# An attention-and-mixing kernel: first batch reordered, u of batch 0 transposed by TensorE, attention woven into nine tenths of mixing

## The chip, the cores and the metric

The kernel runs on one core of a Trainium2 chip. The metric is the device time of one execution in microseconds (us). Most quoted profiles are single executions; their span, from the first to the last instruction, is about 2 us shorter than the time. A run is called fast when it is within 1.5% of the fastest run of the same kernel, slow otherwise.

Engines: TensorE (PE in the profile; its weight loads are PEld), VectorE (DVE), ScalarE (ACT), GpSimd (POOL, here it only issues the loads), SyncE (SP, here it issues output writes and transposes by DMA).

## The reference

Two stages on 4 batches. First attention with 8 heads of 64 over 768 positions, where a query sees the previous 96 positions and the first 8. Then a mixing block on its result x (768 x 512):

```python
theta = x @ w_theta
zr, zi = x * cos(theta), x * sin(theta)
y = einsum('ts,bsd->btd', w_tok_r, zr) + einsum('ts,bsd->btd', w_tok_i, zi)
u = x + y
out = u + maximum(u @ w_ch, 0)
```

## The kernel before

Work comes in tiles of 128 positions (NT = 6 per batch), heads in pairs (NP = 4). `prep` copies a pair's q and k and transposes them on TensorE; `scores` multiplies, exponentiates (ScalarE) and applies a bias table (VectorE); `values` makes x; `xtrans` transposes x; `theta` gives cosine, sine and z; `mix` is the large product (12 matmuls for each of 6 tiles); `utrans` transposes u; `chan` multiplies by w_ch, adds and writes; `trans_w(tt)` transposes the token weights of tile tt; `warm` multiplies zeros, only to keep TensorE's clock up. The attention of batch b+1 is woven into `mix` of batch b. From batch 1 on, x is transposed by DMA; u is transposed by DMA in all batches but for the very last tile.

```python
    # head, VectorE and ScalarE in this order: ramp, ident, dist, the 8 bias tables,
    # e_bufs, grel, gbias, gmask, shift, halfpi, ... (cut)
    etab = const.tile([T, H, W], BF)
    for h in range(H):
        nc.scalar.activation(etab[:, h, :], dist, AF.Exp, scale=-slopes[h])
    # ... (cut)
    def utrans(b, tt):
        u = u_sb[b, tt]
        uT = moe.tile([T, NC, T], BF, name="uT", bufs=4)
        uTs[(b, tt)] = uT
        if (b, tt) != (B - 1, NT - 1):
            nc.sync.dma_start_transpose(out=uT, in_=u)
            return
        ps = ps_small([T, NC, T], BF)
        for dc in range(NC):
            nc.tensor.transpose(ps[:, dc, :], u[:, dc * T:(dc + 1) * T], ident)
        nc.scalar.copy(out=uT, in_=ps)
    # ... (cut)
    load_w()
    load_all(1)
    with tc.manual_schedule(engines={mybir.EngineType.PE}):
        warm(8)
        prep(0, 0)
        warm(2)
        for p in range(1, NP):
            prep(0, p)
            for c in range(NT // 2):
                scores(0, p - 1, c)
                warm(1)
        # ... globals_, vglob, last scores (cut)
        for p in range(NP):
            values(0, p, 0)
            values(0, p, 1)
            if p:
                trans_w(p - 1, nc.scalar.copy)
                xtrans(0, p - 1, nc.scalar.copy)
        trans_w(3, nc.scalar.copy)
        xtrans(0, NP - 1, nc.scalar.copy)
    tail = []
    for b in range(B):
        # ... (cut)
        th[2:2] = tail                 # thetas, with the last chans of batch b-1
        if b:
            th[3:3] = pre              # and the q/k preparation of batch b+1
            pre = []
        weave(th, [])
        # main: mix, with utrans(tt-1) and chan(tt-2) after the first third of tile tt (cut)
        weave(main, pre + side, 0.3 if b == 0 else 0.0)
        tail = [(512, lambda b=b: utrans(b, NT - 1)), (2048, lambda b=b: chan(b, NT - 2)),
                (2048, lambda b=b: chan(b, NT - 1))]
```

Only the head fixes TensorE's order by hand. After it the order is the scheduler's, which may move instructions; the order of this text is a wish.

The softmax here doesn't subtract the row's maximum and nothing guards it: scores larger than these inputs give would overflow.

Of the kernel before, what the change touches and what calls it, by code (L numbers as in the profile page):

```python
# [16 lines left out]
def kernel(  # L17
# [15 lines left out]
    T = 128  # L33
# [29 lines left out]
    def alloc_loads(b):  # L63
        qk = ld.tile([T, 2, H, NT, D], BF, name="qk")
        vn = ld.tile([T, H, NT, D + 1], BF, name="vn")
        nc.vector.memset(vn[:, :, :, D:D + 1], 1.0)
        loads[b] = (qk, vn)
# [17 lines left out]
    load_v(0, 0, 4)  # L85
    load_v(0, 4, 4)

    ones = const.tile([T, W], FP)
# [14 lines left out]
    far = const.tile([T, W], FP)  # L103
    nc.vector.tensor_scalar(far, dist, 0.0, 1e6, op0=ALU.is_lt, op1=ALU.mult)
    nc.vector.tensor_add(dist, dist, far)
    nc.vector.tensor_scalar(far, dist, float(NL), 1e6, op0=ALU.is_ge, op1=ALU.mult)
    nc.vector.tensor_add(dist, dist, far)
    etab = const.tile([T, H, W], BF)
    for h in range(H):
        nc.scalar.activation(etab[:, h, :], dist, AF.Exp, scale=-slopes[h])  # L110


    NE = 4
    e_bufs = []
    for i_ in range(NE):
        e_t = const.tile([T, 2, NT, 2 * T], BF, name=f"e_{i_}")
        nc.vector.memset(e_t[:, :, :, W:2 * T], 0.0)
        e_bufs.append(e_t)
    e_cnt = [0]



    grel = const.tile([T, T], FP)
    nc.vector.tensor_scalar(grel, ramp[:, 0:T], kmod[:, 0:1], None, op0=ALU.subtract)
    gbias = const.tile([T, 2], FP)
    for hh in range(2):
        for p in range(NP):
            nc.vector.memset(gbias[GS * p:GS * (p + 1), hh:hh + 1], -float(NL) * slopes[2 * p + hh])

    gneg = const.tile([T, 1], FP)  # L130
    nc.vector.tensor_scalar(gneg, grel[:, 0:1], -float(NG), -30000.0, op0=ALU.is_le, op1=ALU.mult)
    nc.vector.tensor_scalar(gbias, gbias, gneg, None, op0=ALU.add)

    gfar = const.tile([T, T], FP)
    nc.vector.tensor_scalar(gfar, grel, float(NL), None, op0=ALU.is_ge)
    gmask = const.tile([T, T], BF)
    nc.vector.scalar_tensor_tensor(gmask, in0=grel, scalar=0.0, in1=gfar, op0=ALU.is_lt, op1=ALU.add)

    shift = const.tile([T, NP, T], BF)
    nc.vector.memset(shift, 0.0)  # L140
    for p in range(NP):
        nc.vector.tensor_copy(out=shift[0:NG, p, GS * p:GS * p + NG], in_=ident[0:NG, 0:NG])

    halfpi = const.tile([T, 1], FP)
    nc.vector.memset(halfpi, HALF_PI)

# [23 lines left out]

    zero = const.tile([T, 512], BF)
    nc.vector.memset(zero, 0.0)  # L172

    def warm(n):
# [14 lines left out]

    def prep(b, p):  # L190
        qk = loads[b][0]
# [5 lines left out]
        with behind("dve"):  # L197
            for i_ in range(2):
                nc.vector.tensor_copy(out=qkn[:, :, i_].rearrange("p t h d -> p h t d"),  # L199
                                      in_=qk[:, i_, 2 * p:2 * p + 2])  # L200
        qT = att.tile([T, S], BF, name="qT", bufs=6)
        kT = att.tile([T, S], BF, name="kT", bufs=6)
        for i_, dst in ((0, qT), (1, kT)):
            ps = ps_small([T, NT, T], BF)
            with behind("pe"):
                for t_ in range(NT):
                    nc.tensor.transpose(ps[:, t_, :], qkn[:, t_, i_].rearrange("p h d -> p (h d)"), ident)  # L207

            dst = dst.rearrange("p (n t) -> p n t", t=NT)
            src = ps.rearrange("p t n -> p n t")  # L210
            if i_ == 0:
                nc.vector.tensor_copy(out=dst, in_=src)  # L212
            else:
                nc.scalar.copy(out=dst, in_=src)  # L214
        qkT[(b, p)] = (qT, kT)

# [18 lines left out]
    def scores(b, p, c):  # L235
# [21 lines left out]
        else:  # L257
            nc.scalar.activation(e_t[:, :, jt, 0:W], pb[:, :, 0:W], AF.Exp, scale=scale)
            nc.scalar.activation(e_t[:, :, jt + 1, 0:T], pb[:, :, W:W + T], AF.Exp, scale=scale)
            nc.vector.tensor_mul(e_t[:, :, jt, 0:W], e_t[:, :, jt, 0:W], etab[:, 2 * p:2 * p + 2, :])  # L260
# [79 lines left out]
    def mix(b, tt, g):  # L340
# [8 lines left out]
        if g == NT // 2 - 1:  # L349
            u_sb[b, tt] = moe.tile([T, DM], BF, name="u", bufs=4)  # L350
            anchor["dve"] = nc.vector.tensor_add(  # L351
                u_sb[b, tt].rearrange("p (g d) -> p g d", g=NP), x_sb[b][:, :, tt, :],
                ps.rearrange("p (g d) -> p g d", g=NP)).ins

    def utrans(b, tt):
        u = u_sb[b, tt]
        uT = moe.tile([T, NC, T], BF, name="uT", bufs=4)
        uTs[(b, tt)] = uT
        if (b, tt) != (B - 1, NT - 1):
            nc.sync.dma_start_transpose(out=uT, in_=u)  # L360
            return
# [43 lines left out]

    def weave(main, side, s0=0.0):

# [3 lines left out]
        for w, f in main:  # L411
            f()
            done += w
            while i_ < len(side) and s0 + (1 - s0) * (sdone + side[i_][0] / 2) / stot <= done / total:
                side[i_][1]()
                sdone += side[i_][0]
                i_ += 1
# [6 lines left out]
    with tc.manual_schedule(engines={mybir.EngineType.PE}):  # L424
        warm(8)
        prep(0, 0)
        warm(2)
        for p in range(1, NP):
            prep(0, p)
            for c in range(NT // 2):  # L430
# [3 lines left out]
        for p in range(NP):  # L434
            vglob(0, p)
        for c in range(NT // 2):
            scores(0, NP - 1, c)
            warm(1)
        for p in range(NP):
            values(0, p, 0)  # L440
            values(0, p, 1)
            if p:
                trans_w(p - 1, nc.scalar.copy)
                xtrans(0, p - 1, nc.scalar.copy)
        trans_w(3, nc.scalar.copy)
        xtrans(0, NP - 1, nc.scalar.copy)
    tail = []
    for b in range(B):
        nxt = b + 1 if b + 1 < B else None
        if b + 2 < B:  # L450
            load_all(b + 2)
        th = [(2048, lambda c=c, j=j: theta(b, c, j)) for c in range(NT // 2) for j in range(2)]
        th[2:2] = tail
        pre = [(1536, lambda p=p: prep(nxt, p)) for p in range(NP)] if nxt else []
        if b:
            th[3:3] = pre
            pre = []
        weave(th, [])
        main = []
        for tt in range(NT):  # L460
            for g in range(NT // 2):
                main.append((2048, lambda tt=tt, g=g: mix(b, tt, g)))
                if b == 0 and g == 1 and tt < 2:
                    main.append((1536, lambda tt=tt: trans_w(tt + 4)))
                if tt and g == 0:
                    main.append((0, lambda tt=tt: utrans(b, tt - 1)))
                if tt > 1 and g == 0:
                    main.append((2048, lambda tt=tt: chan(b, tt - 2)))
        side = attention_steps(nxt) if nxt else []
        weave(main, pre + side, 0.3 if b == 0 else 0.0)  # L470
        tail = [(512, lambda b=b: utrans(b, NT - 1)), (2048, lambda b=b: chan(b, NT - 2)),
                (2048, lambda b=b: chan(b, NT - 1))]
    for _, f in tail:
        f()
# [35 lines left out]
```

## Time and profile before

| | before |
|---|---|
| median of its first runs | 201.2 us |
| span of the profiled run | 199.5 us |
| TensorE busy | 173.0 us, 87% |
| head, to the first mixing matmul | 40.35 us |
| mixing 0 | 39.64 us |
| theta of batch 1, 2 | 12.39, 12.40 us |
| mixing 1, 2 | 29.18, 29.54 us |
| theta of batch 3, to the end | 36.00 us |

The stretches end where the first theta matmul or the first mixing matmul of a batch starts in the timeline. This is the view of busy time by stretches for the kernel before: start and end, length, then for each engine busy time and (instructions); then the granted TensorE clock (1 is full), the mean number in which DMA engines were busy, and GB/s.

```profile
core 0: us, PE busy (x) PEld busy (x) DVE busy (x) ACT busy (x) POOL busy (x), PEclk, DMA share, GB/s
0.00:40.35 40.35, 28.83 (x363) 17.61 (x363) 28.44 (x92) 27.13 (x46) 21.43 (x28) 1.00 1.37 175
40.35:79.99 39.64, 35.62 (x372) 18.68 (x373) 28.16 (x62) 21.45 (x32) 3.57 (x3) 1.00 1.77 180
79.99:92.38 12.39, 10.56 (x82) 5.52 (x81) 11.25 (x24) 7.68 (x9) 2.22 (x1) 1.00 1.94 133
92.38:121.56 29.18, 29.18 (x293) 13.63 (x292) 19.62 (x43) 16.71 (x26) 0.00 (x0) 1.00 0.34 89
121.56:133.96 12.40, 10.32 (x82) 5.64 (x81) 9.68 (x20) 7.01 (x8) 0.00 (x0) 1.00 0.34 48
133.96:163.50 29.54, 29.43 (x294) 13.77 (x292) 20.09 (x43) 17.17 (x27) 0.00 (x0) 1.00 0.38 81
163.50:171.12 7.62, 5.69 (x26) 2.19 (x25) 3.02 (x6) 2.91 (x3) 0.00 (x0) 1.00 0.47 116
171.12:199.50 28.38, 23.37 (x108) 10.03 (x107) 12.35 (x23) 4.93 (x6) 0.00 (x0) 1.00 0.28 86
```

Mixing 1 and 2 have TensorE busy all the time. The idle time is in the head, in mixing 0, in the theta stretches and at the end. The Trainium skill, "Perfetto Trace Analysis", Identifying the Most-Contended Engine, warns that matmul busy time is no measure of headroom because matmuls are pipelined. This trace agrees that they are: a 128x512 matmul is shown 380 ns long, but in a dense stretch the next one starts 0.216 us later. So work is better counted in starts: 0.86 us for a chan.

TensorE's waits, longest in total first (line and tile that waited, what it waited for, us in total, times, longest):

```profile
PE ps L177 <- DVE zero L172: 7.8, 1, 7.8
PE ps L371 <- DMA uT<-u: 3.3, 4, 2.1
PE pb L327 <- DMA xT<-x_sb: 3.0, 2, 1.9
PE ps L207 <- DVE qkn L199: 2.0, 2, 1.1
```

L371 is `chan`, L327 is `theta`, L207 is `prep`. The timeline shows the two DMA waits (start, length, engine, line, operation, count, and in brackets the idle time before it and its releaser; lines from two places of the same timeline):

```profile
7.89 0.84 DVE L199 COPY qkn<-qk 128x768 bf16<-128x768 bf16 x1
14.23 1.73 ACT L251 ACTIVATE e_115<-pb 128x896 bf16<-128x896 f32 x2
...
47.10 3.85 SPq L360 DMA_TRANSPOSE uT<-u  x2
54.46 1.04 PE L371 MATMUL ps<-w_ch_bf,uT 128*128 128x512 bf16 x4 [2.07 <-DMA uT<-u]
...
122.15 1.21 SPq L306 DMA_TRANSPOSE xT<-x_sb  x1
126.42 0.82 PE L327 MATMUL pb<-w_theta_bf,xT 128*128 128x512 bf16 x3 [1.91 <-DMA xT<-x_sb]
```

The first u transpose is issued at 47.10 and lands 7.3 us later, although the median of all u transposes is 2.5 us: from about 5 to 80 us the loads keep the DMA engines at 160 to 210 GB/s. The last x transpose of batch 2 is issued when mixing 1 has already ended, and theta waits for it.

### The profile page before, as it was taken

To read this page: it belongs to the slowest core of one execution; us is meant where nothing else is said; L and a number is where in the kernel's file an instruction comes from. 1 tells how busy PE (TensorE), PEld (TensorE's weight loads), DVE (VectorE), ACT (ScalarE), POOL (GpSimd) and SP (SyncE) were. 2 spreads that over 40 slices of the span, in tenths; PEclk is the share of its full clock that TensorE was granted. 3 is DMA by queue.
4 is the path that set the end of the run, shared out by engine and by line. 5 is a ranking of instruction groups with operands and counts; after the bars stand their busy time and mean duration, and the time that the engine had idled before them with its cause. 6 is when DMAs were issued, how large, how long until landed. Compare 5 with 4: busy or idle time off the path is not lost.

```text
span 199.5 us, 3940 instructions
## 1 busy us (share of the span) xinstructions
PE 173.0 (87%) x1610; PEld 87.1 (44%) x1610; DVE 132.6 (66%) x305; ACT 105.0 (53%) x153; POOL 27.2 (14%) x31
## 2 busy tenths in 40 slices
PE   0498789998599899799999999699999997899981
PEld 0154268443353445453345455443444552344430
DVE  7878678177765686996676777677686661753332
ACT  2449956990359553189964431399845312920010
POOL 7991461040110000400000000000000000000000
PEclk9999999999999999999999999999999999999999
DMA  4999999999999999699114437210233845103432
GB/s 66 161 174 168 210 209 206 205 176 166 194 165 188 210 162 183 116 135 138 30 26 118 122 92 108 40 69 37 55 82 100 111 120 123 53 20 100 130 91 105
DMA packets 61345, 24.76 MB, mean 124 GB/s; under 512 B 47504, under 2 KB 58256, under 8 KB 61328
## 3 DMA queue, kind: packets, MB, share of 16 engines
q0 software_dynamic: 35760, 12.85, 66.0%
q1 hardware_dynamic: 25568, 11.67, 26.8%
q8 instruction: 12, 0.20, 0.4%
q14 instruction: 5, 0.04, 0.1%
HBM read 25.69 MB, written 6.29 MB: 160 GB/s over the span
## 4 chain that ended last, share of the span: by engine, by line
PE 61%; DMA 13%; ACT 12%; DVE 9%; issue 3%; ACTq 0%
PE ps L346 27%; DMA uT<-u 11%; PE ps L371 9%; PE pb L327 6%; PE pb L292 6%; PE pb L247 4%; PE ps L207 3%; ACT kT L214 2%; DMA xT<-x_sb 2%; PE ps L177 2%; ACT cs L331 2%; DVE u L351 1%; ACT e_121 L251 1%; PE ps L292 1%; PE ps L167 1%
## 5 line engine op out<-in xcount | busy, mean ns | idle before, releaser
L346 PE MATMUL ps<-zri,w_tokT_151 128*128 128x512 bf16 x144 | 53.9, 380 | 1.2 <-DVE zri L335 1.2
L346 PE MATMUL ps<-zri,w_tokT_152 128*128 128x512 bf16 x144 | 54.0, 379 | 0.1
L374 DVE SCALAR_TENSOR_TENSOR o_sb<-ps,u 128x512 f32<-128x512 f32 x24 | 16.5, 688 | 18.8 <-PE ps L371 18.8
L371 PE MATMUL ps<-w_ch_bf,uT 128*128 128x512 bf16 x96 | 24.7, 379 | 4.1 <-DMA uT<-u 3.3
L327 PE MATMUL pb<-w_theta_bf,xT 128*128 128x512 bf16 x96 | 24.6, 379 | 3.3 <-DMA xT<-x_sb 3.0
L214 ACT COPY kT<-ps 128x768 bf16<-128x768 bf16 x16 | 12.4, 808 | 25.9 <-PE ps L207 25.9
L335 DVE TENSOR_TENSOR zri<-x_sb,cs 128x512 bf16<-128x512 bf16 x48 | 18.2, 421 | 8.8 <-ACT cs L331 7.2
L346 PEld LDWEIGHTS <-w_tokT_151 128*128 128x128 bf16 x144 | 14.0, 97 | 16.9 <-issue 4.4
L351 DVE TENSOR_TENSOR u<-x_sb,ps 128x512 bf16<-128x512 bf16 x24 | 16.4, 684 | 7.0 <-PE ps L346 6.7
L346 PEld LDWEIGHTS <-w_tokT_152 128*128 128x128 bf16 x144 | 14.0, 98 | 12.8 <-issue 2.0
L247 PE MATMUL pb<-qT,kT 64*128 64x224 bf16 x192 | 16.8, 254 | 1.7 <-ACT e_117 L251 0.5
L212 DVE COPY qT<-ps 128x768 bf16<-128x768 bf16 x16 | 14.9, 948 | 2.5 <-PE ps L207 2.5
L177 PE MATMUL ps<-zero 128*128 128x512 bf16 x22 | 8.9, 476 | 8.3 <-DVE zero L172 7.8
L207 PE MATMUL ps<-ident,qkn 128*128 128x128 bf16 x192 | 13.8, 223 | 2.0 <-DVE qkn L199 2.0
L78 POOL DMA_DIRECT2D vn<-in_v_dram x5 | 10.2, 2050 | 35.7 <-DVE rec L300 24.7
L327 PEld LDWEIGHTS <-xT 128*128 128x128 bf16 x96 | 8.8, 98 | 14.1 <-DMA xT<-x_sb 4.1
L207 PEld LDWEIGHTS <-qkn 128*128 128x128 bf16 x192 | 12.1, 100 | 6.4 <-DVE qkn L199 3.8
L371 PEld LDWEIGHTS <-uT 128*128 128x128 bf16 x96 | 8.2, 97 | 14.7 <-DMA uT<-u 6.0
L247 PEld LDWEIGHTS <-kT 64*128 64x128 bf16 x192 | 6.0, 94 | 18.2 <-issue 15.8
L331 ACT ACTIVATE cs<-pb,halfpi 128x1024 bf16<-128x1024 f32 x12 | 13.6, 1131 | 0.5 <-ACT cs L332 0.3
L332 ACT ACTIVATE cs<-pb 128x1024 bf16<-128x1024 f32 x12 | 12.5, 1039 | 0.0
L199 DVE COPY qkn<-qk 128x768 bf16<-128x768 bf16 x32 | 11.5, 411 | 0.8 <-DMA qk<-in_q_dram 0.5
(128 smaller groups left out, 261.8 us busy)
## 6 DMA issues: line engine op xcount, KB each, us to landing
out_dram<-o_sb SPq DMA_DIRECT2D x24, 256.0 KB, 2.2
qk<-in_q_dram POOLq DMA_DIRECT2D x3, 768.0 KB, 17.5
qk<-in_k_dram POOLq DMA_DIRECT2D x3, 768.0 KB, 21.8
vn<-in_v_dram POOLq DMA_DIRECT2D x3, 768.0 KB, 23.3
w_nat<-in_moe_w_tok_r_dram POOLq DMA_DIRECT2D x3, 384.0 KB, 14.7
w_nat<-in_moe_w_tok_i_dram POOLq DMA_DIRECT2D x3, 384.0 KB, 15.9
qk<-in_q_dram POOLq DMA_DIRECT2D x4, 192.0 KB, 5.6
qk<-in_k_dram POOLq DMA_DIRECT2D x4, 192.0 KB, 5.8
```

What stands on the lines that cost most here:

```text
L207: nc.tensor.transpose(ps[:, t_, :], qkn[:, t_, i_].rearrange("p h d -> p (h d)"), ident)
L212: nc.vector.tensor_copy(out=dst, in_=src)
L214: nc.scalar.copy(out=dst, in_=src)
L247: nc.tensor.matmul(pb[:, hh, j * W:j * W + n], lhsT=kT[R, jt * T:(jt + 1) * T], rhs=qT[R, jt * T:jt * T + n], start=True, stop=True)
L292: nc.tensor.matmul(o, lhsT=l_, rhs=r_, start=(i_ == 0), stop=(i_ == len(mms) - 1))
L327: nc.tensor.matmul(pb[:, j, :], lhsT=xT[:, dc, st * T:(st + 1) * T], rhs=w_theta_bf[:, dc, :], start=(dc == 0), stop=(dc == NC - 1))
L331: nc.scalar.activation(cs[:, 0], pb, AF.Sin, bias=halfpi)
L335: nc.vector.tensor_mul(zri[b][:, i_, 2 * c + j_, :].rearrange("p (g d) -> p g d", g=NP), xb[:, :, 2 * c + j_, :], cs[:, i_, j_].rearrange( ...
L346: anchor["pe"] = nc.tensor.matmul(ps, lhsT=w_tokT[wi][:, st, tt * T:(tt + 1) * T], rhs=zri[b][:, wi, st, :], start=(st == 0 and wi == 0), ...
L351: anchor["dve"] = nc.vector.tensor_add(u_sb[b, tt].rearrange("p (g d) -> p g d", g=NP), x_sb[b][:, :, tt, :], ps.rearrange("p (g d) -> p g ...
L371: nc.tensor.matmul(ps_c, lhsT=uT[:, dc, :], rhs=w_ch_bf[:, dc, :], start=(dc == 0), stop=(dc == NC - 1))
L374: nc.vector.scalar_tensor_tensor(o_sb, in0=ps_c, scalar=0.0, in1=u, op0=ALU.max, op1=ALU.add)
```

## The change

Its intent: start the first batch as soon as its first q/k has landed; take the weight transposes out of the head; keep u of batch 0 off the DMA queues while they are full of loads; let attention end before mixing does, so that the last x transpose is hidden; load ScalarE's sine table early; and reorder the boundary between batches. One q/k load buffer instead of two pays for a fifth u buffer.

```diff
-        qk = ld.tile([T, 2, H, NT, D], BF, name="qk")
+        qk = ld.tile([T, 2, H, NT, D], BF, name="qk", bufs=1)
 # ... constants and bias tables become functions, called between the preparations (cut)
-                nc.vector.tensor_copy(out=qkn[:, :, i_].rearrange("p t h d -> p h t d"),
-                                      in_=qk[:, i_, 2 * p:2 * p + 2])
+                (nc.scalar.copy if b == 0 and i_ and p < 2 else nc.vector.tensor_copy)(
+                    out=qkn[:, :, i_].rearrange("p t h d -> p h t d"), in_=qk[:, i_, 2 * p:2 * p + 2])
 # ... scores of the last pair end with a dummy sine:
+            if p == NP - 1:
+                with tc.issue_after(last):
+                    nc.scalar.activation(junk, halfpi, AF.Sin)
-        if (b, tt) != (B - 1, NT - 1):
+        if b and (b, tt) != (B - 1, NT - 1):
             nc.sync.dma_start_transpose(out=uT, in_=u)
-        prep(0, 0)
-        warm(2)
+        prep(0, 0, 4)
+        bias_table(0)
         for p in range(1, NP):
-            prep(0, p)
+            prep(0, p, 2 if p == 1 else 0)
+            bias_table(p)
+            if p == 1:
+                constants()
 # ... last scores go between the values; of trans_w only tile 0 stays in the head (cut)
-        th[2:2] = tail
-        if b:
-            th[3:3] = pre
+        elif nxt:
+            order = rest[:-1] + pre[:2] + th[:2] + pre[2:] + th[2:3] + rest[-1:] + th[3:]
+        else:
+            order = rest[:-1] + th[:3] + rest[-1:] + th[3:]
 # ... batch 0: trans_w(tt+1) and utrans(tt-1) after the second third of tile tt; later batches:
 # utrans(tt) right after tile tt (cut)
-        weave(main, pre + side, 0.3 if b == 0 else 0.0)
+        weave(main, side, 0.3 if b == 0 else 0.0, 0.9)
```

More of the change, by code (lines that the diff above doesn't have):

```diff
@@ L86 @@
     load_v(0, 4, 4)
+    zero = const.tile([T, 512], BF)
+    nc.vector.memset(zero, 0.0)
     ones = const.tile([T, W], FP)
@@ L103 @@
     far = const.tile([T, W], FP)
-    nc.vector.tensor_scalar(far, dist, 0.0, 1e6, op0=ALU.is_lt, op1=ALU.mult)
-    nc.vector.tensor_add(dist, dist, far)
-    nc.vector.tensor_scalar(far, dist, float(NL), 1e6, op0=ALU.is_ge, op1=ALU.mult)
-    nc.vector.tensor_add(dist, dist, far)
+    nc.vector.tensor_scalar(far, dist, 0.0, None, op0=ALU.is_lt)
+    nc.vector.scalar_tensor_tensor(far, in0=dist, scalar=float(NL), in1=far, op0=ALU.is_ge, op1=ALU.add)
+    nc.vector.scalar_tensor_tensor(dist, in0=far, scalar=1e6, in1=dist, op0=ALU.mult, op1=ALU.max)
@@ L108, with bias_table @@
     etab = const.tile([T, H, W], BF)
-    for h in range(H):
-        nc.scalar.activation(etab[:, h, :], dist, AF.Exp, scale=-slopes[h])
+    def bias_table(p):
+        for h in (2 * p, 2 * p + 1):
+            nc.scalar.activation(etab[:, h, :], dist, AF.Exp, scale=-slopes[h])
     NE = 4
-    e_bufs = []
-    for i_ in range(NE):
-        e_t = const.tile([T, 2, NT, 2 * T], BF, name=f"e_{i_}")
-        nc.vector.memset(e_t[:, :, :, W:2 * T], 0.0)
-        e_bufs.append(e_t)
+    e_bufs = [const.tile([T, 2, NT, 2 * T], BF, name=f"e_{i_}") for i_ in range(NE)]
@@ L119 @@
     e_cnt = [0]
-    grel = const.tile([T, T], FP)
-    nc.vector.tensor_scalar(grel, ramp[:, 0:T], kmod[:, 0:1], None, op0=ALU.subtract)
     gbias = const.tile([T, 2], FP)
-    for hh in range(2):
-        for p in range(NP):
-            nc.vector.memset(gbias[GS * p:GS * (p + 1), hh:hh + 1], -float(NL) * slopes[2 * p + hh])
-    gneg = const.tile([T, 1], FP)
-    nc.vector.tensor_scalar(gneg, grel[:, 0:1], -float(NG), -30000.0, op0=ALU.is_le, op1=ALU.mult)
-    nc.vector.tensor_scalar(gbias, gbias, gneg, None, op0=ALU.add)
@@ L134 @@
-    gfar = const.tile([T, T], FP)
-    nc.vector.tensor_scalar(gfar, grel, float(NL), None, op0=ALU.is_ge)
-    gmask = const.tile([T, T], BF)
-    nc.vector.scalar_tensor_tensor(gmask, in0=grel, scalar=0.0, in1=gfar, op0=ALU.is_lt, op1=ALU.add)
-    shift = const.tile([T, NP, T], BF)
-    nc.vector.memset(shift, 0.0)
-    for p in range(NP):
-        nc.vector.tensor_copy(out=shift[0:NG, p, GS * p:GS * p + NG], in_=ident[0:NG, 0:NG])
-    halfpi = const.tile([T, 1], FP)
-    nc.vector.memset(halfpi, HALF_PI)
+    gmask = const.tile([T, T], BF)
@@ new lines, with constants @@
+    shift = const.tile([T, NP, T], BF)
+    halfpi = const.tile([T, 1], FP)
+    junk = const.tile([T, 1], FP)
+    def constants():
+        for e_t in e_bufs:
+            nc.vector.memset(e_t[:, :, :, W:2 * T], 0.0)
+        grel = const.tile([T, T], FP, name="grel")
+        nc.vector.tensor_scalar(grel, ramp[:, 0:T], kmod[:, 0:1], None, op0=ALU.subtract)
+        for hh in range(2):
+            for p in range(NP):
+                nc.vector.memset(gbias[GS * p:GS * (p + 1), hh:hh + 1], -float(NL) * slopes[2 * p + hh])
+        gneg = const.tile([T, 1], FP, name="gneg")
+        nc.vector.tensor_scalar(gneg, grel[:, 0:1], -float(NG), -30000.0, op0=ALU.is_le, op1=ALU.mult)
+        nc.vector.tensor_scalar(gbias, gbias, gneg, None, op0=ALU.add)
+        gfar = const.tile([T, T], FP, name="gfar")
+        nc.vector.tensor_scalar(gfar, grel, float(NL), None, op0=ALU.is_ge)
+        nc.vector.scalar_tensor_tensor(gmask, in0=grel, scalar=0.0, in1=gfar, op0=ALU.is_lt, op1=ALU.add)
+        nc.vector.memset(shift, 0.0)
+        for p in range(NP):
+            nc.vector.tensor_copy(out=shift[0:NG, p, GS * p:GS * p + NG], in_=ident[0:NG, 0:NG])
+        nc.vector.memset(halfpi, HALF_PI)
@@ L168, in trans_w @@
             (copy if wi else nc.vector.tensor_copy)(out=w_tokT[wi][:, :, tt * T:(tt + 1) * T], in_=ps)
-    zero = const.tile([T, 512], BF)
-    nc.vector.memset(zero, 0.0)
     def warm(n):
@@ L188, in behind, with prep @@
         return tc.issue_after(anchor[eng]) if eng in anchor else nullcontext()
-    def prep(b, p):
+    def prep(b, p, w=0):
         qk = loads[b][0]
@@ L214, in prep @@
                 nc.scalar.copy(out=dst, in_=src)
+            if w:
+                warm(w)
         qkT[(b, p)] = (qT, kT)
@@ L258, in scores @@
             nc.scalar.activation(e_t[:, :, jt, 0:W], pb[:, :, 0:W], AF.Exp, scale=scale)
-            nc.scalar.activation(e_t[:, :, jt + 1, 0:T], pb[:, :, W:W + T], AF.Exp, scale=scale)
+            last = nc.scalar.activation(e_t[:, :, jt + 1, 0:T], pb[:, :, W:W + T], AF.Exp, scale=scale).ins
+            if p == NP - 1:
+                with tc.issue_after(last):
+                    nc.scalar.activation(junk, halfpi, AF.Sin)
             nc.vector.tensor_mul(e_t[:, :, jt, 0:W], e_t[:, :, jt, 0:W], etab[:, 2 * p:2 * p + 2, :])
@@ L349, in mix @@
         if g == NT // 2 - 1:
-            u_sb[b, tt] = moe.tile([T, DM], BF, name="u", bufs=4)
+            u_sb[b, tt] = moe.tile([T, DM], BF, name="u", bufs=5)
             anchor["dve"] = nc.vector.tensor_add(
@@ L404, in attention_steps, with weave @@
         return steps
-    def weave(main, side, s0=0.0):
+    def weave(main, side, s0=0.0, s1=1.0):
         total = float(sum(w for w, _ in main)) or 1.0
@@ L413, in weave @@
             done += w
-            while i_ < len(side) and s0 + (1 - s0) * (sdone + side[i_][0] / 2) / stot <= done / total:
+            while i_ < len(side) and s0 + (s1 - s0) * (sdone + side[i_][0] / 2) / stot <= done / total:
                 side[i_][1]()
@@ L435 @@
             vglob(0, p)
-        for c in range(NT // 2):
-            scores(0, NP - 1, c)
-            warm(1)
+        scores(0, NP - 1, 0)
         for p in range(NP):
@@ L441 @@
             values(0, p, 1)
+            if p < 2:
+                scores(0, NP - 1, p + 1)
             if p:
-                trans_w(p - 1, nc.scalar.copy)
                 xtrans(0, p - 1, nc.scalar.copy)
-        trans_w(3, nc.scalar.copy)
         xtrans(0, NP - 1, nc.scalar.copy)
-    tail = []
+        trans_w(0, nc.scalar.copy)
+    rest = []
     for b in range(B):
@@ L451 @@
             load_all(b + 2)
-        th = [(2048, lambda c=c, j=j: theta(b, c, j)) for c in range(NT // 2) for j in range(2)]
-        th[2:2] = tail
-        pre = [(1536, lambda p=p: prep(nxt, p)) for p in range(NP)] if nxt else []
-        if b:
-            th[3:3] = pre
-            pre = []
-        weave(th, [])
+        lag = 2
+        th = [lambda c=c, j=j: theta(b, c, j) for c in range(NT // 2) for j in range(2)]
+        pre = [lambda p=p: prep(nxt, p) for p in range(NP)] if nxt else []
+        if b == 0:
+            order = th
+        elif nxt:
+            order = rest[:-1] + pre[:2] + th[:2] + pre[2:] + th[2:3] + rest[-1:] + th[3:]
+        else:
+            order = rest[:-1] + th[:3] + rest[-1:] + th[3:]
+        for f in order:
+            f()
         main = []
@@ L462 @@
                 main.append((2048, lambda tt=tt, g=g: mix(b, tt, g)))
-                if b == 0 and g == 1 and tt < 2:
-                    main.append((1536, lambda tt=tt: trans_w(tt + 4)))
-                if tt and g == 0:
-                    main.append((0, lambda tt=tt: utrans(b, tt - 1)))
-                if tt > 1 and g == 0:
-                    main.append((2048, lambda tt=tt: chan(b, tt - 2)))
-        side = attention_steps(nxt) if nxt else []
-        weave(main, pre + side, 0.3 if b == 0 else 0.0)
-        tail = [(512, lambda b=b: utrans(b, NT - 1)), (2048, lambda b=b: chan(b, NT - 2)),
-                (2048, lambda b=b: chan(b, NT - 1))]
-    for _, f in tail:
+                if b == 0 and g == 1 and tt + 1 < NT:
+                    main.append((1536, lambda tt=tt: trans_w(tt + 1)))
+                if tt >= lag and g == 0:
+                    main.append((2048, lambda tt=tt: chan(b, tt - lag)))
+                if b == 0 and tt and g == 1:
+                    main.append((512, lambda tt=tt: utrans(b, tt - 1)))
+            if b:
+                main.append((0, lambda tt=tt: utrans(b, tt)))
+        side = [(1536, f) for f in pre] if b == 0 else []
+        side += attention_steps(nxt) if nxt else []
+        weave(main, side, 0.3 if b == 0 else 0.0, 0.9)
+        rest = [lambda tt=tt, b=b: chan(b, tt) for tt in range(NT - lag, NT)]
+        if b == 0:
+            rest.insert(1, lambda b=b: utrans(b, NT - 1))
+    for f in rest:
         f()
```

## The prediction

> **What bounds the kernel now.** From the 201.2 us runs I read a span of 199.5 us. The table by stretches splits it: first batch before mixing, 0 to 40.3 us, TensorE busy 28.8; mixing of batch 0 with attention of batch 1 woven in, 40.3 to 80.0, TensorE 35.6 of 39.7; theta of batch 1, 12.5 us; mixing 1, 28.7 of 28.7 busy; theta of batch 2, 12.2 of 14.4; mixing 2, 27.9 of 27.9; the end from 163.5, 29.1 of 36.0. So mixing 1 and 2 are bound by TensorE and can't shrink; everything to be won is in the first 80 us and in the two gaps and the end. The timeline shows them: scores of the first batch paced by ScalarE (a pair of heads every 3.04 us), theta waiting until 37.4 for xT copies queued behind the token-weight copies, u transposes by DMA that land after 7.3 and 8.7 us while loads fill the queues (later ones take 2.5), an xT transpose issued at 122.15 and awaited at 126.4, another at 164.1.
>
> **Head.** The first pair of q/k is copied as soon as it lands (about 7 us, estimate from 1.3 plus 5.6), half of it by ScalarE, instead of after all constants. But TensorE's eight warm-up matmuls now end near 5 us and it then waits for data; the Trainium skill, "TensorE: Matmul & The Clock Gate", HAM clock gate, says the clock falls back after about 3.4 us idle. The trace agrees that first matmuls are slow (0.43 us, later 0.22), so the extra warm matmuls cost about 0.43 each. The eight bias-table exponentials (0.29 us each) now sit inside ScalarE's chain. I expect the first scores exponential at about 13.8 (was 14.2), and the third pair to end no earlier than before. The gain comes after it: values start while the last scores run, three of four early weight transposes leave (twelve transposes and 0.65 us each, with 0.8 us ScalarE copies), and the sine table load (1.28 us) is paid before the copies. VectorE now paces: eight reciprocals and multiplies (0.63 each) plus last table products 1.9 from 25.5, then an xT copy: theta's rest starts at 33.8, first cosine at 35.3 instead of 38.7. About -3.4 us.
>
> **Mixing 0.** Adds three weight transposes (2.0 us TensorE, 3.3 VectorE copies) and six PE transposes of u (about 1.3 TensorE, 3.5 ScalarE); removes DMA waits of 2.1 and 0.75 us and some of the slack. After the first u I count 30.4 us TensorE work to theta 1, where 30.4 passed before; with VectorE fuller I allow 1.5 us new waits. Theta 1 near 77.5 (was 80.0): cumulative -2.5.
>
> **Later.** Attention ends at nine tenths of mixing, so the last xT transpose lands before theta: theta 2 about 12.6 instead of 14.4 us (-1.8); end stage about 1.8 shorter (theta 3 no longer waits 1.05 and 0.27, nor the sine load 1.28). One q/k buffer: batch 2's load issues near 48 us (was 28.8), but isn't needed until about 76; batch 3's not until 118. Free, by my count.
>
> Sum: -2.5 -0.2 -1.8 -1.8, about -6.5: **194.6 us**, range 191.3 to 198.5. Faster by over 2%: 0.8; within: 0.18; slower: 0.02.
>
> **Signs.** TensorE busy rises slightly; no u transpose by DMA before about 90; the weight-from-xT waits on DMA vanish; theta 2's stretch has TensorE above 95%; mixing 1 and 2 stay 28 us.
>
> **What would make it wrong.** Batch 1's q/k landing after 46 us; small-PSUM rotation in mixing 0 stalling TensorE behind VectorE or ScalarE copies by more than 3 us; a cold TensorE clock delaying the first scores; batch 2's q/k landing after 76.

## The result and the profile after

The changed kernel took 193.3 us (median of four runs, 192.08 to 194.72) against 201.4; ratio 0.9598, 95% interval 0.9528 to 0.9667. All ratios here are the mean time of one kernel's fast runs over that of the other's in the same rounds, so they are not quite the ratio of the medians quoted. The profiled run is the fastest of the four (192.08 us, span 190.0), so the 9.5 us between the two profiles are more than the 8 us between the medians.

| stretch | before | after | difference |
|---|---|---|---|
| head, to the first mixing matmul | 40.35 | 35.71 | -4.64 |
| mixing 0 | 39.64 | 41.73 | +2.09 |
| theta 1 and mixing 1 | 41.57 | 39.57 | -2.00 |
| theta 2 and mixing 2 | 41.94 | 40.17 | -1.77 |
| theta 3, mixing 3, end | 36.00 | 32.82 | -3.18 |
| sum | 199.50 | 190.00 | -9.50 |

Theta and mixing are summed because one chan of 0.86 us moved from behind to before the mark at which each theta starts. So 0.86 of the +2.09 of mixing 0, and 0.86 of the -3.18 at the end, are moved work; the two rows between lose one chan and gain another. The same view of stretches, of the changed kernel:

```profile
core 0: us, PE busy (x) PEld busy (x) DVE busy (x) ACT busy (x) POOL busy (x), PEclk, DMA share, GB/s
0.00:35.71 35.71, 28.43 (x332) 16.09 (x334) 25.12 (x86) 26.60 (x46) 21.26 (x26) 1.00 1.38 171
35.71:77.44 41.73, 40.28 (x435) 23.23 (x444) 33.54 (x72) 25.78 (x40) 3.96 (x3) 1.00 1.75 152
77.44:86.27 8.83, 8.70 (x72) 4.92 (x71) 7.94 (x19) 6.81 (x9) 1.75 (x2) 1.00 1.63 134
86.27:117.01 30.74, 30.25 (x293) 14.31 (x296) 21.12 (x45) 17.91 (x28) 0.00 (x0) 1.00 0.72 130
117.01:126.11 9.10, 8.99 (x75) 5.04 (x76) 8.92 (x20) 6.67 (x8) 0.00 (x0) 1.00 0.24 72
126.11:157.18 31.07, 30.15 (x292) 14.22 (x296) 20.57 (x42) 17.70 (x28) 0.00 (x0) 1.00 0.35 84
157.18:163.22 6.04, 6.04 (x29) 2.74 (x28) 3.05 (x7) 3.50 (x4) 0.00 (x0) 1.00 0.44 142
163.22:190.00 26.78, 21.56 (x99) 9.28 (x99) 11.00 (x20) 3.06 (x4) 0.00 (x0) 1.00 0.29 84
```

TensorE is now busy for 96% of mixing 0 and 98 to 100% of each theta stretch. Its waits, longest in total first; L177 is `warm`, L377 is now `chan`; no wait of theta for xT is left:

```profile
PE ps L177 <- DVE zero L88: 1.4, 1, 1.4
...
PE ps L377 <- DMA uT<-u: 0.6, 2, 0.4
```

The places in the timeline that answer to those shown of before:

```profile
4.73 0.39 DVE L199 COPY qkn<-qk 128x768 bf16<-128x768 bf16 x1 [1.52 <-DMA qk<-in_q_dram]
12.59 1.71 ACT L253 ACTIVATE e_108<-pb 128x896 bf16<-128x896 f32 x2
...
43.63 0.39 PE L370 MATMUL ps<-ident,u 128*128 128x128 bf16 x4
44.05 0.59 ACT L371 COPY uT<-ps 128x512 bf16<-128x512 bf16 x1 [3.88 <-PE ps L370]
...
114.83 1.21 SPq L312 DMA_TRANSPOSE xT<-x_sb  x1
117.01 0.38 PE L333 MATMUL pb<-w_theta_bf,xT 128*128 128x512 bf16 x1
```

The first copy starts 3.2 us earlier and the first scores exponential 1.6 us earlier. The first u is transposed and copied within about a microsecond, where the DMA took 7.3. The last x transpose of batch 2 now goes out 2.2 us before its theta starts. Of the prediction's signs four came true (TensorE busy 174.4 us against 173.0, the first u transpose by DMA at 90.87, no theta wait for xT, theta 2 busy for 99%); the fifth did not: mixing 1 and 2 are 30.74 and 31.07 us instead of 28, 0.86 of the growth by the moved chan.

### The profile page after: what moved, and what is told of

The parts are those of the page before. It is cut to its first block, busy times and chain, and to the rows that moved or that the text cites. A ratio compares the mean times of both kernels' runs of the same rounds, so it can differ in the third digit from the quotient of the medians.

```text
span 190.0 us, 3965 instructions
## 1 busy us (share of the span) xinstructions
PE 174.4 (92%) x1616; PEld 89.8 (47%) x1641; DVE 131.3 (69%) x305; ACT 108.0 (57%) x162; POOL 27.0 (14%) x31
## 4 chain that ended last, share of the span: by engine, by line
PE 65%; ACT 15%; DVE 8%; DMA 6%; issue 3%; POOL 1%; ACTq 0%; SPq 0%; POOLq 0%
PE ps L352 27%; PE ps L377 10%; PE pb L333 9%; PE pb L298 7%; PE pb L249 5%; DMA uT<-u 3%; PE ps L207 3%; DMA qk<-in_k_dram 3%; ACT cs L337 2%; ACT kT L214 2%; ACT e_108 L253 2%; PE ps L170 2%; DVE qT L212 1%; DVE qkn L199 1%; DVE zri L341 1%
## 5 line engine op out<-in xcount | busy, mean ns | idle before, releaser
L352 PE MATMUL ps<-zri,w_tokT_119 128*128 128x512 bf16 x136 | 51.6, 381 | 1.2 <-DVE zri L341 0.5
L352 PE MATMUL ps<-zri,w_tokT_120 128*128 128x512 bf16 x138 | 52.2, 379 | 0.5 <-issue 0.2
L377 PE MATMUL ps<-w_ch_bf,uT 128*128 128x512 bf16 x89 | 23.5, 380 | 1.2 <-DMA uT<-u 0.6
L333 PE MATMUL pb<-w_theta_bf,xT 128*128 128x512 bf16 x93 | 23.2, 379 | 0.2
L214 ACT COPY kT<-ps 128x768 bf16<-128x768 bf16 x16 | 12.9, 806 | 12.9 <-PE ps L207 12.8
L352 PEld LDWEIGHTS <-w_tokT_120 128*128 128x128 bf16 x144 | 14.1, 98 | 12.5 <-issue 1.4
L371 ACT COPY uT<-ps 128x512 bf16<-128x512 bf16 x7 | 4.1, 587 | 27.0 <-PE ps L370 27.0
L207 PE MATMUL ps<-ident,qkn 128*128 128x128 bf16 x192 | 15.0, 222 | 0.9 <-DVE ident L101 0.4
L78 POOL DMA_DIRECT2D vn<-in_v_dram x5 | 9.5, 1921 | 24.9 <-DVE rec L306 20.9
L377 PEld LDWEIGHTS <-uT 128*128 128x128 bf16 x96 | 8.1, 98 | 10.4 <-DMA uT<-u 2.1
L199 DVE COPY qkn<-qk 128x768 bf16<-128x768 bf16 x30 | 10.8, 387 | 3.1 <-DMA qk<-in_q_dram 3.1
L177 PE MATMUL ps<-zero 128*128 128x512 bf16 x28 | 10.4, 473 | 2.4 <-DVE zero L88 1.4
```

The costliest lines, as they stand in the source:

```text
L207: nc.tensor.transpose(ps[:, t_, :], qkn[:, t_, i_].rearrange("p h d -> p (h d)"), ident)
L214: nc.scalar.copy(out=dst, in_=src)
L333: nc.tensor.matmul(pb[:, j, :], lhsT=xT[:, dc, st * T:(st + 1) * T], rhs=w_theta_bf[:, dc, :], start=(dc == 0), stop=(dc == NC - 1))
L352: anchor["pe"] = nc.tensor.matmul(ps, lhsT=w_tokT[wi][:, st, tt * T:(tt + 1) * T], rhs=zri[b][:, wi, st, :], start=(st == 0 and wi == 0), ...
L377: nc.tensor.matmul(ps_c, lhsT=uT[:, dc, :], rhs=w_ch_bf[:, dc, :], start=(dc == 0), stop=(dc == NC - 1))
```

## The experiments

Twelve kernels ran, all correct. The table gathers them; ratios are to the kernel before in the same rounds. They ran in three groups (r0, e1, e2, e3; f1, e4, e5, e6, on another chip; h2, h3, i1, g2), so runs of different groups are compared by their ratios.

| run | what it is | fast mean, us | ratio | 95% interval |
|---|---|---|---|---|
| r0_after | changed kernel | 194.07 | 0.9601 | 0.9550 to 0.9653 |
| e1_u_by_dma | changed, u of batch 0 by DMA | 202.51 | 1.0019 | 0.9970 to 1.0068 |
| i1_dma_u_two_qk | the same, two q/k buffers | 203.17 (one run) | none | |
| f1_only_pe_u | before, u of batch 0 by TensorE | 197.55 | 0.9791 | 0.9752 to 0.9831 |
| h2_new_head_only | f1 and the new head | 195.50 | 0.9701 | 0.9653 to 0.9748 |
| h3_old_head | f1 and the new boundaries | 195.50 | 0.9701 | 0.9655 to 0.9747 |
| e2_weave_full | changed, attention over all of mixing | 194.83 | 0.9625 | 0.9583 to 0.9667 |
| e4_no_early_sine | changed, no early sine | 194.07 | 0.9626 | 0.9574 to 0.9678 |
| e5_old_bounds | changed, old order at boundaries | 193.73 | 0.9602 | 0.9564 to 0.9640 |
| e6_consts_first | changed, constants first | 194.64 | 0.9647 | 0.9602 to 0.9693 |
| e3_two_qk | changed, two q/k buffers | 193.59 | 0.9578 | 0.9535 to 0.9620 |
| g2_end_order_warm | attempt at a better one | 193.94 | 0.9623 | 0.9574 to 0.9672 |

### r0_after: the yardstick

No edit.

> The changed kernel itself, as the yardstick of this group. Both theories: ratio to before 0.960, about 193 us, span near 190 to 191; theta of batch 1 starts near 77.4, first mixing matmul near 35.7.

Ratio 0.9601 in its fast runs. Its profiled run was a slow one, 241.5 us at a mean granted clock of 0.753, and is left out. The fast runs spread with the granted clock. Taking the changed kernel's nine fast runs together: three at 0.997 or more average 192.8 us, four at 0.986 to 0.991 average 193.8, two at 0.982 average 195.1. In the kept profiles, this slow one apart, every dip of the clock after the start of the kernel is of one kind: half speed for 3.41 us, as in the next experiment. The slow one is another state, with 0.75 granted over nearly all of its span.

### e1_u_by_dma: the TensorE transposes undone

```diff
-        if b and (b, tt) != (B - 1, NT - 1):
+        if (b, tt) != (B - 1, NT - 1):
-                if b == 0 and tt and g == 1:
-                    main.append((512, lambda tt=tt: utrans(b, tt - 1)))
-            if b:
-                main.append((0, lambda tt=tt: utrans(b, tt)))
+            main.append((0, lambda tt=tt: utrans(b, tt)))
-        if b == 0:
-            rest.insert(1, lambda b=b: utrans(b, NT - 1))
```

> Changed kernel, but u of batch 0 transposed by DMA as before (issued right after each u). Theory (transposes issued into the load traffic land after 7 to 9 us, chan waits for them): theta of batch 1 starts 2 to 4 us later than in the changed kernel, total 195.5 to 197. Rival (the TensorE transposes cost 1.3 us of TensorE, 3.5 us of ScalarE and PSUM buffers, as much as the waits that they remove): within 0.7 us of the changed kernel.

The five fast runs took 201.4 to 203.4 us: 8.4 us more than the changed kernel, the whole gain, and twice the upper end of what I expected. The profile fell in a run of 206.2 us, which counts as slow, so its sizes are not those of the fast runs, and the account below is not shown for them; it shows where to look. What the fast runs do show is the clock: 0.974 to 0.988, on average 0.979 against 0.990 in those of r0. By an estimate from these two means the clock is about 2 of the 8.4 us. Lines of its timeline, in two places:

```profile
43.58 4.13 SPq L366 DMA_TRANSPOSE uT<-u  x2
51.15 0.61 PE L377 MATMUL ps<-w_ch_bf,uT 128*128 128x512 bf16 x1 [3.49 <-DMA uT<-u]
...
79.56 2.22 POOL L78 DMA_DIRECT2D vn<-in_v_dram  x1 [20.55 <-DVE rec L306]
79.78 1.13 SPq L382 DMA_DIRECT2D out_dram<-o_sb  x1
81.00 1.27 SPq L312 DMA_TRANSPOSE xT<-x_sb  x1
88.33 1.03 PE L333 MATMUL pb<-w_theta_bf,xT 128*128 128x512 bf16 x2 [3.64 <-DMA xT<-x_sb]
```

and the busy view in pieces around the first wait:

```profile
47.10:50.60 3.50, 0.56 (x11) 0.39 (x7) 1.60 (x4) 0.80 (x1) 0.00 (x0) 1.00 3.14 133
50.60:54.00 3.40, 2.63 (x14) 1.75 (x16) 0.93 (x2) 0.00 (x0) 0.00 (x0) 0.51 2.12 154
54.00:57.40 3.40, 3.40 (x37) 2.19 (x36) 2.54 (x6) 2.17 (x3) 0.14 (x1) 0.99 0.56 98
```

Three things are to be seen. First, mixing starts 3.5 us earlier than before and the first u transpose is issued 3.5 us earlier, but it still takes 7.5 us among the loads (7.3 before). It lands 3.3 us earlier, at 51.1 instead of 54.4, so up to here most of the lead is kept, although TensorE waits 3.5 us instead of 2.1. The lead is lost after it: theta 1 starts at 82.97, 3.0 us later than before (79.99), after three more weight transposes (2.0 us), the moved chan (0.86), a second wait for uT (1.35) and the slow clock. Second, TensorE idles for 3.5 us and is then granted half its clock for the next 3.4 us, while its matmuls start twice as far apart. The Trainium skill, "TensorE: Matmul & The Clock Gate", The HAM clock gate, states exactly this: the clock gate falls to half after an idle window of about 3.4 us, and the windows run freely. This trace agrees in length and factor. So does e6_consts_first, whose profile is of a fast run: after a wait of 3.8 us it shows 0.50 from 8.3 to 11.7 us. A half-speed window lowers the mean clock of a 190 us run by 3.4 x 0.5 / 190 = 0.009, which is about the step by which the clocks of the runs differ. Third, the last x transpose of batch 1 is issued 1.4 us after batch 3's v load began, lands after 7.3 us, and theta 1 waits 3.6 us. In the changed kernel it goes out only 0.6 us after the v load began (75.25 and 74.66) and theta starts 2.2 us later without a wait. That the v load slows it is argued from these times, not shown by a run that moves the load.

### i1_dma_u_two_qk: is it the single buffer?

The edit of e1_u_by_dma, and `name="qk")` without `bufs=1`.

> As the run with u of batch 0 by DMA (202.5 us in its fast runs, but its profile fell in a slow run), with two q/k buffers. Theory (the 8 us come from chan 0 waiting for a landing near 51 us that the loads set, the half-speed clock after that wait, and the last xT transpose of batch 1 behind a u transpose in the queue and in batch 3's v load; the number of buffers has no part): 201 to 203.5 us; a wait of 3 us or more for uT near 48 us, a clock below 1 after it, and a wait for xT of 2 us or more at theta 1. Rival (the late load of batch 2's q/k with one buffer is what hurts when transposes go by DMA): 196 to 199.5 us.

One fast run of 203.2 us, and three of 206.3 to 207.2 us that count as slow because they are over 1.5% above it; there is no interval. All four lie above 201, so the rival's 196 to 199.5 us is out. The profile, again of a slow run, has a longest wait for uT of 4.5 us, the clock at half from 52.9 to 56.3 us after it, and a wait for xT of 3.6 us. The second buffer doesn't repair it.

### f1_only_pe_u: the TensorE transposes alone

Edit on the kernel before:

```diff
-        if (b, tt) != (B - 1, NT - 1):
+        if b and (b, tt) != (B - 1, NT - 1):
-                if tt and g == 0:
-                    main.append((0, lambda tt=tt: utrans(b, tt - 1)))
+                if tt and g == (1 if b == 0 else 0):
+                    main.append((512 if b == 0 else 0, lambda tt=tt: utrans(b, tt - 1)))
```

> The kernel before, with one part of the change alone: u of batch 0 transposed by TensorE. Undoing this part in the changed kernel cost all of its gain (ratio 1.0019). Theory (the parts depend on each other: an earlier head only helps if chan no longer waits for transposes whose landing is set by the load traffic): alone it gives the waits of before back, 2.1 and 0.75 us, some of the late xT transposes, less 1.3 us of TensorE: 197.5 to 200.5 us, ratio 0.975 to 0.99. Rival (this part is the whole change): ratio 0.955 to 0.965, about 193.5 us.

Ratio 0.9791, 197.5 us, at the lower edge of the theory's range: this part alone brings half of the gain (it is clearly faster, but the interval leaves open whether by 2%). Undone in the changed kernel it costs 0.042, alone it brings 0.021. The difference is what the other parts lose without it: with u by DMA, the new head and boundaries bring nothing over the kernel before (1.0019); with u by TensorE they bring 0.019.

### h2_new_head_only and h3_old_head: a square of head and boundaries

h2 is the changed kernel with the batch loop of before (attention over all of mixing, old order, old place of utrans, no early sine); weight transposes and u of batch 0 as in the changed kernel:

```diff
-        weave(main, side, 0.3 if b == 0 else 0.0, 0.9)
+        weave(main, pre + side, 0.3 if b == 0 else 0.0)
-            order = rest[:-1] + pre[:2] + th[:2] + pre[2:] + th[2:3] + rest[-1:] + th[3:]
+        th[2:2] = tail
+        if b:
+            th[3:3] = pre
```

> Changed kernel with the whole batch loop as before (attention over all of mixing, old order at the boundaries, no early sine, u transposed after the next block's first third), but u of batch 0 still by TensorE and the new head kept. With the kernel that has only the TensorE transposes (0.979), the changed kernel (0.960) and the next one this makes a square of head and boundaries. Theory (each boundary measure alone was worth nothing because any one of them covers the late xT transpose; all undone it shows; and the head's early start is used up in batch 0's mixing): 197 to 199 us, ratio 0.977 to 0.987, boundary stretches 11 to 12 us again. Rival (the measures are worth the sum of their single effects, about 0.5 per cent, and the head is worth the rest): 194 to 195.5 us, ratio 0.962 to 0.968.

h3 is the kernel before up to the batch loop, with the loop of the changed kernel, the early sine and u of batch 0 by TensorE:

```diff
     warm(8); prep(0, 0); warm(2)          # head as before, constants ahead of it
-    for b in range(B):                    # loop of before
+    for b in range(B):                    # loop of the change, trans_w(4), (5) in mixing only
```

> The kernel before with its old head (constants first, four weight transposes in the head, last scores before values), with the new boundaries, nine tenths, early sine and TensorE transposes of u. Theory (the head's gain of 4.6 us at the first mixing matmul is given back, since the weight transposes, chan and stalls move into mixing 0): within 1.2 us of the changed kernel, ratio 0.958 to 0.967, first mixing matmul at 40, but theta 1 within 1 us of 77.4. Rival (an earlier start is kept to the end): 196.5 us or more, ratio 0.973 or more, theta 1 at 79 or later.

Both came out at 0.9701. With f1 (0.9791, neither) and the changed kernel (0.9601, both) the square is even: the head brings 0.009, the boundaries bring 0.009, together 0.019. Each ratio is known to about 0.005, so 0.009 is above zero, but not by much. Both of my theories missed, and both had valued the head too low; h2 fell next to its rival's range (0.962 to 0.968), h3 between theory and rival. I had said that the head's gain is given back; about 1.8 us of it stays. And I had expected more of the boundaries. Of the head's 4.6 us, h3's profile shows the rest of the account: first mixing matmul at 40.25, theta 1 at 79.88 against 77.44 in the changed kernel (its profile has one half-speed window, that of the changed kernel none).

### e2, e4 and e5: the boundary measures undone one at a time

```diff
-        weave(main, side, 0.3 if b == 0 else 0.0, 0.9)
+        weave(main, side, 0.3 if b == 0 else 0.0, 1.0)
```

> Changed kernel, attention woven into the whole of mixing instead of nine tenths. Theory (the last xT transpose by DMA, about 2.7 us, then ends inside the theta stretch): TensorE waits for xT come back at theta 2 and 3, 1 us or more each, total 1.5 to 4 us longer. Rival (the gaps went because of the order at the boundaries, the early u transposes and the early sine load): within 0.5 us.

Ratio 0.9625. The profile does show waits for xT (1.5 us in 2 times) and for uT (1.6 us in 2 times) again, as the theory said, and theta stretches of 11.97 us and 9.14 us (8.83 and 9.10 in the changed kernel), but the total is within 1 us of the changed kernel.

```diff
-            if p == NP - 1:
-                with tc.issue_after(last):
-                    nc.scalar.activation(junk, halfpi, AF.Sin)
```

> Changed kernel without the dummy sine that loads the table early (1.28 us per load, four loads). Theory: the load stands in front of the first cosine of each batch; TensorE has the rest of theta and chan to run meanwhile, so 0.3 to 0.9 us each, 1.2 to 3 us in all. Rival (it was hidden in any case): within 0.6 us.

Ratio 0.9626: the rival's "within 0.6 us" fits (194.07 against 194.07 of r0, though in another group).

```diff
-            order = rest[:-1] + pre[:2] + th[:2] + pre[2:] + th[2:3] + rest[-1:] + th[3:]
+            order = th[:2] + pre + rest + th[2:]
-            order = rest[:-1] + th[:3] + rest[-1:] + th[3:]
+            order = th[:2] + rest + th[2:]
```

> Changed kernel with the old order of work at the batch boundaries (two thetas first, then q/k preparation, then the last two chan, then theta). Theory (nine tenths alone was worth only about 0.5 us; what shortened theta 1 and 2 from 12.4 to about 9 us is the order, which keeps TensorE fed while the last xT transpose lands): 2 to 4 us longer, TensorE waits for xT and for q/k copies come back at each boundary. Rival (the early ends of attention do it): within 0.7 us.

Ratio 0.9602, no change; the theory of the order fell. In its profile the mixing stretches became shorter as the theta stretches became longer (11.13 us for theta 1, but 29.68 for mixing 1, where the changed kernel has 8.83 and 30.74).

The three single losses add up to 0.005 and undoing all (with the place of utrans in the later batches, which no run undoes alone) costs 0.010, as h2 shows. With intervals of 0.005 on each this doesn't tell "any one of them covers for the others" from "each is worth a little". It stays open.

### e6_consts_first: the constants ahead again

```diff
-        bias_table(0)
-            bias_table(p)
-            if p == 1:
-                constants()
+    for p in range(NP):
+        bias_table(p)
+    constants()
     load_w()
```

> Changed kernel with all constants and all eight bias-table exponentials ahead of the first preparation, as before. Theory (the early start is worth 1.6 us at the first scores exponential, but each pair of heads then needs 0.3 us less of ScalarE): first mixing matmul 0.3 to 1.3 us later than 35.7, total within 1.3 us. Rival (this reordering is what brings the head's 4.6 us): first mixing matmul at 38.5 or later, total 2.5 us or more longer.

Ratio 0.9647, not clearly different from 0.9601. The first mixing matmul was at 37.23, 1.5 us later than in the changed kernel's profile, but this profile has a half-speed window in the head and that one has none, as e2 and e5 also have one and show 37.1 with the early start. The line that changed is TensorE's wait for the first copy:

```profile
PE ps L207 <- DVE qkn L199: 3.8, 1, 3.8
```

So starting TensorE early is worth less than it looks; ScalarE, which starts a pair of heads every 3.02 us when the tables are made first and every 3.25 in the changed kernel, makes up for part of it. e6 loses 0.0046, about half of the head's 0.009 and not clear of zero. How the 0.009 divides between the early start and the second half of the head (weight transposes moved, last scores between values) stays open.

### e3_two_qk: is one buffer free?

```diff
-        qk = ld.tile([T, 2, H, NT, D], BF, name="qk", bufs=1)
+        qk = ld.tile([T, 2, H, NT, D], BF, name="qk")
```

> Changed kernel with two q/k load buffers; the order on TensorE, VectorE, ScalarE and SyncE is the same. Theory (one buffer is free, batch 2's load has slack): within 0.5 us of the changed kernel; batch 2's q issue near 29 us instead of 53. Rival 1 (late loads cost): 1 us or more faster. Rival 2 (early loads fill the DMA queues and slow batch 1's xT transposes to 6 to 9 us, so that theta 1 waits): 1 us or more slower.

Ratio 0.9578, the same within the interval. Batch 2's q load is issued at 51.97 us in the changed kernel (28.75 before) and is wanted at 76.5. One buffer is free, within this interval.

### g2_end_order_warm: an attempt at a better version

```diff
-            if b:
+            if b and (b, tt) != (B - 1, NT - 1):
                 main.append((0, lambda tt=tt: utrans(b, tt)))
-        if b == 0:
+        if b in (0, B - 1):
             rest.insert(1, lambda b=b: utrans(b, NT - 1))
         globals_(0)
+        warm(3)
```

> An attempt at a better version: the changed kernel, with the last but one chan ahead of the last u's transposes (TensorE idles 0.8 us there, and its uT has landed), and three warm-up matmuls after the first batch's global scores, where TensorE waits for ScalarE and some runs show the clock at half. Theory: 0.8 us from the end and 0 to 1 us from the head's clock: ratio 0.951 to 0.957. Rival (the end is bound by u, transposes and the last chan, and the warm matmuls delay the value matmuls): within 0.4 us of the changed kernel, ratio 0.958 to 0.963.

Ratio 0.9623: no better. The last matmuls show why, first in the changed kernel, then in this one:

```profile
183.22 0.69 DVE L357 TENSOR_TENSOR u<-x_sb,ps 128x512 bf16<-128x512 bf16 x1 [1.04 <-PE ps L352]
183.96 0.40 PE L370 MATMUL ps<-ident,u 128*128 128x128 bf16 x4 [0.78 <-DVE u L357]
184.19 1.89 PE L377 MATMUL ps<-w_ch_bf,uT 128*128 128x512 bf16 x8
186.12 0.69 DVE L380 SCALAR_TENSOR_TENSOR o_sb<-ps,u 128x512 f32<-128x512 f32 x1 [0.17 <-PE ps L377]
```

```profile
186.04 0.69 DVE L357 TENSOR_TENSOR u<-x_sb,ps 128x512 bf16<-128x512 bf16 x1 [1.04 <-PE ps L352]
187.01 0.39 PE L370 MATMUL ps<-ident,u 128*128 128x128 bf16 x4
188.08 1.04 PE L377 MATMUL ps<-w_ch_bf,uT 128*128 128x512 bf16 x4 [0.68 <-ACT uT L371]
189.15 0.69 DVE L380 SCALAR_TENSOR_TENSOR o_sb<-ps,u 128x512 f32<-128x512 f32 x1 [1.25 <-PE ps L377]
```

In the changed kernel the last but one chan hides ScalarE's copy of the last uT; moved ahead it hides VectorE's u instead, and TensorE waits 0.68 us for the copy. From the last u to the last output tile it takes 3.11 us instead of 2.90. The warm matmuls didn't keep the clock up either: the half-speed window is there, at 24.1 to 27.5 us. The rival's range, 0.958 to 0.963, holds. No version that ran beats the changed kernel clearly.

## Why the prediction was right, and where it was not

The time (194.6 us predicted, 193.3 measured): right. The sum was right in part by luck: the start of theta 1 came out right because two errors of 1.2 us cancel (head -3.4 predicted, -4.6 measured; mixing 0 +0.9 predicted, +2.1 measured). Point by point:

- **Head.** Predicted -3.4 us at the first cosine (35.3); measured 34.08, -4.6. Two terms were mis-sized. I took 5.6 us, the median of four loads, for the first landing ("about 7 us"), but the first of them is copied at 4.73. And the warm clock is not lost: the transposes start at 5.36, 0.4 us after the warm matmuls end, so the fall of the clock that I feared doesn't come in this profile. It can come: i1 has the same head, and in its profile TensorE waits 1.8 us for the second copy and then gets half its clock from 8.6 to 12.0 us. "The third pair ends no earlier than before" was wrong by 1.1 us. On the other hand, e6 finds no clear loss without the early start.
- **Mixing 0.** Theta 1 predicted at 77.5, measured 77.44. The start was right, its reason was not. I wrote "I count 30.4 us TensorE work to theta 1, where 30.4 passed before". My count, which the prediction doesn't spell out, took 24 transposes for a `prep`; there are 12 (192 in all for 16 preparations), so both counts were too high. Recounted, from the first q/k transpose of batch 1 to theta 1 the changed kernel has 43 mixing matmuls (9.3 us), 5 chan (4.3), 4 prep (2.6), 3 weight tiles (2.0), 5 u transposes (1.1) and attention (8.9), about 28.2 us by estimate, in 31.5 us: 3.3 are left. The kernel before has 48 mixing matmuls (10.4), 4 chan (3.4), 4 prep (2.6) and the same attention, 25.3 us in 30.0: 4.7 are left, 2.8 of them the two waits for uT that the change removes. So the work grew by 2.9 us, where I had it equal, and the remainder beside those waits by about 1.4, near the 1.5 that I allowed.
- **Theta 1.** This is the step that failed: I put theta 1 with mixing 1 at -0.2 us, naming no gap in its 12.5 us. With the right count it is 5.2 (theta's 24 matmuls) + 2.6 + 1.7 = 9.5 us of work, so there were nearly 3 us to be won, and 2.0 were.
- **Theta 2 and the end.** -1.8 predicted, -1.77 measured (my 14.4 us for theta 2 ended later than the table's mark; the differences can be compared); for the end -1.8 predicted, -3.18 measured (0.86 of it is the chan that moved ahead of the mark). I gave the gain to the nine tenths and, in the end stage, to the sine load; neither undone alone costs a clear amount.
- **u by TensorE.** I valued it at the two waits of 2.1 and 0.75 us less its own work, about 1.5 us. It is worth 4.3 us alone and 8.4 us within the change. What I left out is that a long wait can also cost the clock, about 2 us of the 8.4 by the estimate at e1. The rest is read from slow profiles alone (longer waits for uT, and 3.6 us for xT), so how the 8.4 us divide stays open.
- **One q/k buffer.** "Free, by my count": confirmed by e3, and not the cause of e1's loss, by i1.

## What to carry to other kernels

When TensorE waits for transfers that other traffic slows, changes elsewhere can come to nothing, as the new head and boundaries did here with u by DMA (ratio 1.0019): mend that wait first, or measure the other parts only together with it. Undo a part in the new kernel and try it alone in the old one; where the two numbers differ, as 8.4 and 4.3 us here, the parts depend on each other. And after a wait of some three microseconds on TensorE look at the granted clock too: here waits of 3.5 us (e1) and 3.8 us (e6) were each followed by 3.4 us at half speed.

## What the Trainium skill lacked or had wrong

- "DMA: Bandwidth & Descriptors", Latency and other measured facts: it gives a bandwidth for transposes by DMA, but no time of one small transpose from SBUF to SBUF, idle or among loads. Here one of 128x512 landed after 2.4 us at best, and 8.7 us at worst while the loads ran.
- The same page, Issuing engines are not separate DMA queues: it calls the sequencer's issue time usually small beside the DMA. Here SyncE spent 1.2 us to issue one transpose that lands 2.4 us after the issue begins, half of the whole.
- "ScalarE: Activation LUTs", What ACT_TABLE_LOAD costs: it gives about 1.28 us for the load and about 1.38 us more for a drain. The load itself is 1.28 us here too, but in the changed kernel the exponential before it ends at 71.01, the load starts at 71.03 and the sine starts at 72.32: 1.31 us in all, no drain to be seen.
- "TensorE: Matmul & The Clock Gate", The HAM clock gate: length and factor are as it says (3.41 us, half), but it names an idle window as what makes the clock fall; a later section of the page lets frequent short idle times do it too, without a measure. In the profile of g2 TensorE was shown busy for 2.16 of the 3.41 us before the half-speed window in the head, and e1, e2, e5 and h3 show 2.32 to 2.47 us there. What decides it these runs don't show.
- The same section tells of variation from run to run in the cold matmuls at a kernel's start, but not of whole half-speed windows that come and go later. Here the changed kernel's fast runs go from 192.1 to 195.5 us with clocks of 1.0 to 0.982, which is zero to two such windows by the estimate at e1, although TensorE's longest wait in its profile is 1.4 us.
